# Two chunks per turn of the main loop of a retention-and-SoLU kernel, with a new order of its ends

## The chip, the core and the metric

One of the eight cores of a Trainium2 chip runs the whole kernel. A core has a matrix engine (TensorE, PE in the profile, with its weight loads as PEld), three engines for elementwise work (VectorE or DVE, ScalarE or ACT, GpSimd or POOL) and SyncE (SP), which here only issues DMAs. Each engine works through its own queue in order. Matrix products land in PSUM, which has eight banks; everything else works in SBUF. The metric is the time of one execution on the device, in microseconds (us).

## What is computed

q, k and v have 8 batches, 8 heads, 576 positions and 64 columns. Retention weights the scores of a head by a power of that head's gamma, with nothing from later positions; the result of all heads, 512 wide, goes through a SoLU layer, a layer norm and a second matrix.

```
scores = q @ k.T / sqrt(64)
gamma  = 1 - 2 ** (-5 - head)
ret    = (scores * where(i >= j, gamma ** (i - j), 0)) @ v
x      = ret, heads side by side                # 4608 x 512
h      = x @ w_in                               # 4608 x 1024
e      = exp(h - max(h));  solu = h * e / sum(e)
ln     = (solu - mean) / sqrt(var + 1e-6) * g_ln
out    = ln @ w_out                             # 4608 x 512
```

## The kernel before

The 4608 positions are cut into 36 chunks of 128. Batches go in pairs: chunks of the two batches alternate for four chunks each, and the last 64 positions of both make a ninth, joint chunk (position 4 in its batch). Along a batch a state (a 64 by 64 matrix per head) is carried from chunk to chunk, so a chunk depends on the chunk two before it.

The whole order of work is written by hand. START, LOOP and END are lists of tokens `name:chunk:engine`; `run` goes through a list and calls the function of that name, and each engine's queue gets its instructions in the order of the list. START names its chunks outright; LOOP is run once for each i from FIRST, with chunk numbers counted from i; END counts from the last chunk, 35. The letter at the end picks the engine where a step can run on several: a for ScalarE, v for VectorE, g for GpSimd.

The steps of one chunk, with their lines in the profile:

- `ld` loads q, k and v (SP, L169). `cq` and `cv` scale q and v by powers of gamma and make them half precision (L176), `ck` casts k (L160).
- `tq` transposes q and k on PE (L199), `eq` copies the result to SBUF (L160). `sc` multiplies keys and queries, head by head (L223: 64 rows of the array per product, two products side by side), `mk` puts the triangular mask on, in two instructions on DVE (L236).
- `kv` makes the chunk's product of keys and values (L247: 64 columns of the array per product), `ad` adds it to the state on DVE (L260, L262), `dk` and `d3` scale the state on POOL (L274, L286). The joint chunk has none of these.
- `av` multiplies the masked scores by v (L298: 64 columns), `fs` adds the part that comes from the state (L313: the full array); `ex` copies the sum to SBUF (L160).
- `m1` is the product with w_in (L345, eight products of 512 columns), `mx` its negative maximum (DVE, L355), `xp` the exponential (ACT, L361), `so` h times e with its sum (DVE, L370), `ce` takes the mean off (DVE, L379 and L384, in place), `sq` sums the squares (ACT, L393), `rt` makes the row factor on POOL in three small instructions (L402, L405, L406).
- `tu` transposes the result (L414), `eu` copies it to SBUF (L160), `m2` multiplies by w_out (L428), `st` scales the output (ACT, L436) and stores it (SP, L441).

`mr` is a piece of `m1` used at the start, when the rows of w_in come in one after the other; `hm` to `hw` do the last chunk in halves; `li`, `wi`, `lo`, `wo` load the weights and make them half precision; `wu` is a dummy product.

PSUM is shared out by hand too: `m1` has two slots of two banks, and all other products take one of four single banks, in the order in which the digits of BANKS name them. A product waits until the last user of its bank has been read.

Before, FIRST is 7, STEP 1 and STOP 32: a turn of the loop is one chunk's worth of every step, taken from different chunks, and there are 25 turns.

Of the kernel before, what the change touches and what calls it, by code (L numbers as in the profile page):

```python
# [10 lines left out]
FP = mybir.dt.float32  # L11
F16 = mybir.dt.float16
P = 128
H = 8
D = 64
# [1 line left out]

FIRST = 7  # L20
STEP = 1
STOP = 32
START = """
ld:1 c1:0 cq:1:g ck:1:a tq:1 ld:0 ld:2 cq:2:g eq:1:v ck:0:v ck:2:g cv:0:v cq:0:v sc:1 li:3
mk:1 tq:0 cv:1:g eq:0:v sc:0 kv:0 mk:0 kv:1 av:1 wi:3:0:a tq:2 cv:2:g kv:2 ad:1 eq:2:v
wi:3:1:g li:2 li:0 d3:1 dk:1 li:1 ad:0 fs:1 av:0 ld:4 ld:3 ex:1:a wi:0:1:v wi:2:1:v wi:2:0:v
fs:0 mr:1:3 wi:1:1:g d3:0 sc:2 ex:0:v wi:0:0:a mk:2 mr:1:0 mr:1:2 wi:1:0:a mr:1:1 mr:0:0
cq:4:g ck:4:a ad:2 mr:0:2 dk:0 mx:1 mr:0:1 ld:5 tq:4 eq:4:v mr:0:3 xp:1 d3:2 av:2 sc:4 fs:2
c2:0 wu:0:5 cv:4:g mx:0 ex:2:a cq:3:g ld:6 so:1 xp:0 ck:3:a ce:1 sq:1 lo:2 kv:4 m1:2 mk:4 so:0
dk:2 tq:3 av:4 eq:3:a cv:3:g kv:3 fs:4 ex:4:a ck:5:a cq:5:g mx:2 tu:1 cv:5:g tq:5 xp:2 ad:4  # L30
lo:1 eu:1:a sc:3 ad:3 ce:0 m1:4 mk:3 av:3 cq:6:g eq:5:a so:2 ck:6:a dk:3 d3:3 fs:3 mx:4 ex:3:a
d3:4 cv:6:g sc:5 tq:6 sq:0 d3:6 kv:5 m1:3 ce:2 lo:3 lo:0 eq:6:a tu:2 dk:4 mk:5 ad:5 sc:6 kv:6
wo:5:g av:5 xp:4 wo:4:a fs:5 mk:6 eu:2:a ld:7 so:4 ex:5:a wo:3:a wo:7:a tu:0 av:6 eu:0:v
wo:2:a wo:1:a ce:4 d3:5 wo:6:g cq:7:g rt:1 sq:4 wo:0:v rt:0 cv:7:g sq:2 fs:6 rt:4 m1:5 tu:4
mx:3 ad:6 xp:3 m2:0 eu:4:v ld:8 ld:9 ex:6:a m2:1 dk:5 mx:5 cq:8:g m2:4 ck:7:v so:3 tq:7 dk:6
ce:3 tu:3 xp:5 st:0 m1:6 kv:7 so:5 sq:3 eq:7:v ck:8:v eu:3:v sc:7 ad:7 ce:5 ld:10 st:1 mx:6
ld:11 st:4 tq:8 rt:2 ld:12 cv:8:v eq:8:a mk:7 m2:2 m2:3 ck:9:a sc:8 xp:6 rt:3 st:2 av:7 cq:9:g
mk:8 cq:10:g fs:7 st:3 ex:7:a ck:10:v cv:9:g
"""
LOOP = """  # L40
tu:-2 so:-1 tq:2 dk:0 d3:0 eq:2:a eu:-2:a ce:-1 m1:0 kv:1 ad:1 av:1 sc:2 mx:0 sq:-2 mk:2 fs:1
ex:1:a rt:-2 cq:4:g xp:0 ld:6 m2:-2 st:-2 cv:3:v ck:4:g
"""
END = """
d3:-3 dk:-3 so:-4 cv:0:g tq:-1 m1:-3 eq:-1:a d3:-2 kv:-2 av:-2 ad:-2 sq:-5 sc:-1 fs:-2 mk:-1
tq:0 ex:-2:a tu:-5 eq:0:a mx:-3 eu:-5:a m1:-2 kv:-1 ce:-4 mx:-2 xp:-3 av:-1 fs:-1 ex:-1:a
so:-3 m2:-5 sc:0 kv:0 ad:-1 ce:-3 dk:-2 xp:-2 mk:0 so:-2 rt:-5 m1:-1 av:0 dk:-1 sq:-4 mx:-1
st:-5 sq:-3 fs:0 ex:0:a tu:-3 rt:-4 tu:-4 hm:0:0 eu:-4:a ce:-2 hm:0:1 eu:-3:a xp:-1 tu:-2
rt:-3 hx:0:0 m2:-3 hx:0:1 hp:0:0 eu:-2:v m2:-4 hp:0:1 st:-3 so:-1 ce:-1 sq:-2 ho:0:1 ho:0:0
tu:-1 rt:-2 d3:-1 m2:-2 hc:0 sq:-1 eu:-1:v ht:0:1 st:-4 ht:0:0 rt:-1 hq:0:0:v m2:-1 he:0:0:v  # L50
he:0:1:a hq:0:1:a st:-2 st:-1 rt:0 h2:0:0 hw:0:0:a h2:0:1 hw:0:1:v ad:0
"""

BANKS = """
012301230130120123010230213103210231230231203012303120312013201302130210321032013201302130210321
032013201302130210321032013201230123021302132013201230123021302132013201230123021302132013203120
3123012301320132031203123012301320132013021301203123030213013
"""


# [25 lines left out]
def kernel(  # L86
# [66 lines left out]
    def bank(shape, dtype, name):  # L153
        return ps.tile(shape, dtype, tag="b" + next(banks), name=name)

    ENG = {"a": nc.scalar, "v": nc.vector, "g": nc.gpsimd}
    T = {}
# [78 lines left out]
            nc.vector.tensor_tensor(out=r, in0=s, in1=m, op=ALU.mult)  # L236
            T["ret", n].append(r)

    def kv(n):

        k16, v16 = T.pop(("k16", n)), T["v16", n]
        if chunks[n][1] == 4:
            return
        kp = bank([P, 4, D], FP, "kp")
        for hp in range(4):
            for e in range(2):
                nc.tensor.matmul(  # L247
                    out=kp[64 * e : 64 * e + 64, hp], lhsT=k16[:, 2 * hp + e],
                    rhs=v16[:, 2 * hp + e], start=True, stop=True,
                )  # L250
        T["kp", n] = kp
# [370 lines left out]
    def run(order, base):  # L622

        for token in order.split():
            name, n, *more = token.split(":")
            n = base + int(n)
            if 0 <= n < NCH:
                step[name](n, *more)

    with tc.manual_schedule():  # L630
        run(START, 0)
        for i in range(FIRST, STOP - STEP + 1, STEP):
            run(LOOP, i)
# [31 lines left out]
```

## Time and profile before

| | us |
|---|---|
| median of 3 runs | 223.36 (222.85 to 224.05) |
| the profiled execution, its own time | 223.33 |
| its span in the profile | 221.5 |
| PE busy in it | 203.6 (92%) |
| DVE busy | 196.2 (89%) |
| ACT busy | 186.6 (84%) |
| POOL busy | 163.8 (74%) |
| mean granted clock of TensorE | 0.998 |

The span runs from the first to the last instruction in the profile; the device's own time is 1.8 us more. Busy shares are sums over stages, and neighbouring instructions of one engine overlap a little at their ends, so an instruction's cost to its engine is best read from its start to the start of the next where nothing is waited for.

### The profile page before, as it was taken

To read this page: it belongs to the slowest core of one execution; us is meant where nothing else is said; L and a number is where in the kernel's file an instruction comes from. 1 tells how busy PE (TensorE), PEld (TensorE's weight loads), DVE (VectorE), ACT (ScalarE), POOL (GpSimd) and SP (SyncE) were. 2 spreads that over 40 slices of the span, in tenths; PEclk is the share of its full clock that TensorE was granted. 3 is DMA by queue.
4 is the path that set the end of the run, shared out by engine and by line. 5 is a ranking of instruction groups with operands and counts; after the bars stand their busy time and mean duration, and the time that the engine had idled before them with its cause. 6 is when DMAs were issued, how large, how long until landed. Compare 5 with 4: busy or idle time off the path is not lost.

```text
span 221.5 us, 5624 instructions
## 1 busy us (share of the span) xinstructions
PE 203.6 (92%) x2125; PEld 117.8 (53%) x2125; DVE 196.2 (89%) x343; ACT 186.6 (84%) x294; POOL 163.8 (74%) x245
## 2 busy tenths in 40 slices
PE   0269989999999999999999999999999999999992
PEld 0144455555655555555555555555555555554552
DVE  0288899999899999999999999999999999989970
ACT  2112799997899999999999999999999999998982
POOL 2077879699659988887759988887759988895050
PEclk9999999999999999999999999999999999999999
DMA  7999999889999996999897967998897945111024
GB/s 150 212 307 307 206 226 337 207 177 254 269 241 262 215 244 158 247 250 223 174 241 176 209 140 188 256 204 191 183 207 174 210 99 143 50 47 52 0 96 142
DMA packets 121084, 42.50 MB, mean 192 GB/s; under 512 B 114657, under 2 KB 115041, under 8 KB 121057
## 3 DMA queue, kind: packets, MB, share of 16 engines
q1 hardware_dynamic: 119424, 41.82, 81.5%
q10 hardware_dynamic: 1632, 0.32, 0.9%
q8 instruction: 16, 0.26, 0.6%
q14 instruction: 12, 0.09, 0.2%
HBM read 32.70 MB, written 9.44 MB: 190 GB/s over the span
## 4 chain that ended last, share of the span: by engine, by line
PE 81%; DVE 6%; SPq 6%; DMA 4%; issue 1%; ACT 0%; DVEq 0%
PE o L428 27%; PE h L345 24%; PE lp L414 7%; PE tp L199 6%; PE sc L223 5%; SPq L169 5%; PE x L313 4%; DMA kf<-in_k_dram 4%; PE x L298 4%; PE kp L247 3%; DVE ret L236 1%; DVE u L370 1%; DVE nm L355 1%; DVE u L384 1%; SPq L590 1%
## 5 line engine op out<-in xcount | busy, mean ns | idle before, releaser
L428 PE MATMUL o<-w_out,uT 128*128 128x512 f16 x280 | 65.5, 379 | 0.2
L345 PE MATMUL h<-w_in,xT 128*128 128x512 f16 x264 | 62.4, 379 | 0.2 <-DVE u L370 0.2
L236 DVE TENSOR_TENSOR ret<-sc,tris 128x512 f16<-128x512 f32 x72 | 46.1, 681 | 1.7 <-PE sc L223 1.6
L176 POOL TENSOR_TENSOR q<-qf,small 128x512 f16<-128x512 f32 x35 | 36.9, 1056 | 12.1 <-DMA qf<-in_q_dram 11.9
L361 ACT ACTIVATE e<-h,nm 128x1024 f32<-128x1024 f32 x35 | 39.1, 1117 | 4.8 <-DVE nm L355 4.6
L370 DVE SCALAR_TENSOR_TENSOR u<-h,e 128x1024 f16<-128x1024 f32 x35 | 42.4, 1211 | 0.4 <-ACT e L361 0.4
L355 DVE TENSOR_REDUCE nm<-h 128x1 f32<-128x1024 f32 x35 | 42.6, 1216 | 0.1
L428 PEld LDWEIGHTS <-uT 128*128 128x128 f16 x280 | 26.2, 98 | 26.5
L393 ACT ACTIVATE sq<-u 128x1024 f16<-128x1024 f16 x35 | 37.4, 1068 | 0.9 <-DVE u L384 0.8
L345 PEld LDWEIGHTS <-xT 128*128 128x128 f16 x264 | 24.3, 98 | 23.9 <-issue 0.2
L274 POOL TENSOR_TENSOR s<-t,small 128x512 f16<-128x512 f32 x32 | 33.7, 1054 | 2.5 <-DVE nmu L379 2.5
L160 ACT COPY qkT<-tp 128x1024 f16<-128x1024 f16 x31 | 31.4, 1012 | 3.0 <-PE tp L199 2.2
L160 ACT COPY uT<-lp 128x1024 f16<-128x1024 f16 x30 | 30.4, 1018 | 0.3 <-PE lp L414 0.3
L405 POOL TENSOR_TENSOR w<-w,ss 128x1 f32<-128x1 f32 x36 | 6.8, 190 | 29.3 <-ACT sq L393 28.4
L160 POOL CAST k<-kf 128x512 f16<-128x512 f32 x26 | 27.4, 1054 | 0.2 <-DMA kf<-in_k_dram 0.2
L436 ACT ACTIVATE o_sb<-o,rs 128x512 f32<-128x512 f32 x35 | 23.7, 680 | 0.6 <-PE o L428 0.4
L199 PE MATMUL tp<-ident,q 128*128 128x128 f16 x144 | 14.6, 226 | 8.8 <-POOL q L176 5.1
L406 POOL TENSOR_TENSOR rs<-w,mhalf 128x1 f32<-128x1 f32 x36 | 20.6, 571 | 2.8
L160 ACT CAST xT<-x 128x512 f16<-128x512 f32 x35 | 20.5, 585 | 2.5 <-PE x L313 2.3
L176 DVE TENSOR_TENSOR v<-vf,small 128x512 f16<-128x512 f32 x27 | 21.9, 812 | 0.8 <-DMA vf<-in_v_dram 0.8
L414 PEld LDWEIGHTS <-u 128*128 128x128 f16 x280 | 18.3, 98 | 6.9 <-issue 0.2
L414 PE MATMUL lp<-ident,u 128*128 128x128 f16 x280 | 21.2, 219 | 0.0
(70 smaller groups left out, 264.1 us busy)
## 6 DMA issues: line engine op xcount, KB each, us to landing
qf<-in_q_dram SPq DMA_DIRECT2D x32, 256.0 KB, 4.3
kf<-in_k_dram SPq DMA_DIRECT2D x32, 256.0 KB, 4.9
vf<-in_v_dram SPq DMA_DIRECT2D x32, 256.0 KB, 4.8
out_dram<-o_sb SPq DMA_DIRECT2D x32, 256.0 KB, 3.0
w_in<-in_moe_w_in_dram SPq DMA_DIRECT2D x4, 512.0 KB, 5.6
w_out<-in_moe_w_out_dram SPq DMA_DIRECT2D x4, 512.0 KB, 7.8
qf<-in_q_dram SPq DMA_DIRECT2D x8, 128.0 KB, 3.6
kf<-in_k_dram SPq DMA_DIRECT2D x8, 128.0 KB, 3.5
```

The source lines that it names most:

```text
L160: (engine.copy if engine is nc.scalar else engine.tensor_copy)(out=out, in_=in_)
L176: engine.tensor_tensor(out=dst, in0=T.pop((key, n)), in1=table.unsqueeze(2).to_broadcast([P, H, D]), op=ALU.mult,)
L199: nc.tensor.transpose(out=tp[:, i, hp], in_=s2[:, hp * P : (hp + 1) * P], identity=ident)
L236: nc.vector.tensor_tensor(out=r, in0=s, in1=m, op=ALU.mult)
L274: nc.gpsimd.tensor_tensor(out=s16, in0=t.unsqueeze(2).to_broadcast([P, 4, 2, D]), in1=gd.unsqueeze(3).to_broadcast([P, 4, 2, D]), op=ALU.mult,
L345: nc.tensor.matmul(out=h[:, i * 512 : (i + 1) * 512], lhsT=xT[:, d], rhs=w_in16[:, d, i * 512 : (i + 1) * 512], start=d == 0, stop=d == 3,)
L355: nc.vector.tensor_reduce(out=nm, in_=T["h", n], axis=AX.X, op=ALU.max, negate=True)
L361: nc.scalar.activation(out=e, in_=T["h", n], func=ACT.Exp, bias=T.pop(("nm", n)), accum_out=s)
L370: nc.vector.scalar_tensor_tensor(out=u, in0=T.pop(("h", n)), scalar=1.0, in1=T.pop(("e", n)), op0=ALU.mult, op1=ALU.mult, accum_out=su,)
L393: nc.scalar.activation(out=s, in_=T.pop(("v", n)), func=ACT.Square, accum_out=ss)
L414: nc.tensor.transpose(out=lp[:, c], in_=u[:, c * P : (c + 1) * P], identity=ident)
L428: nc.tensor.matmul(out=o, lhsT=uT[:, c], rhs=w_out16[:, c], start=c == 0, stop=c == NF - 1)
```

## The change

A turn of the loop takes two chunks, i + 1 and i + 2 (STEP 2, ten turns from 9 to 27). Products that use the array in the same shape stand side by side: `kv` and `av` of both chunks, then the full-array steps, then `sc` of both chunks between the two `m1`. The `kv` of the second chunk writes the second half of the bank that the first one took. The engines of some steps change: in a turn the scaling of v goes from DVE to POOL, and one of two `ex`, one of two `eq` and one of two `eu` go from ACT to DVE; one of two `ck` goes from POOL to ACT. START now covers the first nine chunks and END the last six, both in a new order (among others, a quarter of w_in is loaded ahead of the first chunk), with a new list of banks.

```diff
-FIRST = 7
-STEP = 1
-STOP = 32
+FIRST = 9
+STEP = 2
+STOP = 29
 START = """
-ld:1 c1:0 cq:1:g ck:1:a tq:1 ld:0 ld:2 cq:2:g eq:1:v ck:0:v ck:2:g cv:0:v cq:0:v sc:1 li:3
-mk:1 tq:0 cv:1:g eq:0:v sc:0 kv:0 mk:0 kv:1 av:1 wi:3:0:a tq:2 cv:2:g kv:2 ad:1 eq:2:v
-wi:3:1:g li:2 li:0 d3:1 dk:1 li:1 ad:0 fs:1 av:0 ld:4 ld:3 ex:1:a wi:0:1:v wi:2:1:v wi:2:0:v
-fs:0 mr:1:3 wi:1:1:g d3:0 sc:2 ex:0:v wi:0:0:a mk:2 mr:1:0 mr:1:2 wi:1:0:a mr:1:1 mr:0:0
-cq:4:g ck:4:a ad:2 mr:0:2 dk:0 mx:1 mr:0:1 ld:5 tq:4 eq:4:v mr:0:3 xp:1 d3:2 av:2 sc:4 fs:2
-c2:0 wu:0:5 cv:4:g mx:0 ex:2:a cq:3:g ld:6 so:1 xp:0 ck:3:a ce:1 sq:1 lo:2 kv:4 m1:2 mk:4 so:0
...
+li:2 c1:0 ld:0 cq:0:v ck:0:g tq:0 ld:1 li:1 ck:1:a cv:0:g wi:2:1:g ld:2 eq:0:a li:0 wi:2:0:v
+cq:1:v tq:1 cv:1:v sc:0 mk:0 kv:1 eq:1:v sc:1 mk:1 kv:0 av:0 wi:1:0:g wi:1:1:g cq:2:g av:1
+ad:1 cv:2:g ad:0 ck:2:a d3:0 fs:0 li:3 fs:1 dk:1 ex:1:v tq:2 mr:1:2 mr:1:1 ex:0:v eq:2:a
+wi:0:0:a sc:2 ld:4 dk:0 cq:4:g wi:3:1:a ld:3 kv:2 wi:3:0:v d3:1 wi:0:1:a mr:1:0 ck:4:a mr:0:1
+mr:1:3 cv:4:g mr:0:2 ad:2 mr:0:0 mr:0:3 mk:2 dk:2 mx:1 wu:0:3 tq:4 d3:2 av:2 fs:2 ld:5 ck:3:g
+cq:3:g mx:0 xp:1 ld:6 so:1 eq:4:a cv:3:g cq:5:g ex:2:a sc:4 ce:1 kv:4 m1:2 ck:5:g tq:3 xp:0
+mk:4 ad:4 av:4 mx:2 lo:2 fs:4 sq:1 so:0 eq:3:a sc:3 ex:4:a xp:2 lo:3 c2:0 cv:5:g kv:3 ce:0
+ad:3 d3:4 mk:3 sq:0 tq:5 m1:4 av:3 cq:6:g fs:3 tu:0 d3:3 eq:5:a ck:6:a tq:6 lo:1 ex:3:a sc:5
+so:2 rt:0 mx:4 ce:2 eq:6:a m1:3 mk:5 dk:3 sc:6 kv:5 mk:6 dk:8 eu:0:a cv:6:g tu:1 ad:5 xp:4
+wo:5:a lo:0 so:4 dk:4 wo:7:g av:5 fs:5 ex:5:a kv:6 wo:6:v wo:2:g tu:2 av:6 ad:6 eu:1:a wo:3:a
+fs:6 wo:4:a wo:0:a ex:6:a m1:5 ce:4 wo:1:v mx:3 tu:4 ld:7 eu:4:v xp:3 ld:8 ld:9 mx:5 m2:1 rt:1
...
 LOOP = """
-tu:-2 so:-1 tq:2 dk:0 d3:0 eq:2:a eu:-2:a ce:-1 m1:0 kv:1 ad:1 av:1 sc:2 mx:0 sq:-2 mk:2 fs:1
-ex:1:a rt:-2 cq:4:g xp:0 ld:6 m2:-2 st:-2 cv:3:v ck:4:g
+ld:7 kv:1 kv:2:s ad:2 ad:1 av:1 av:2 dk:1 cv:4:g fs:1 tq:3 tq:4 ex:1:v fs:2 so:0 eq:3:v eq:4:a
+ce:0 ld:8 rt:-1 m1:1 mx:1 sc:3 sc:4 ex:2:a m1:2 sq:0 mk:4 tu:0 d3:1 mx:2 xp:1 eu:0:a dk:2 so:1
+m2:-1 d3:2 ck:6:a xp:2 cv:3:g ce:1 st:-1 cq:5:g rt:0 m2:0 tu:1 st:0 mk:3 ck:5:g eu:1:v cq:6:g
+sq:1
 """
 END = """
...
+ck:-1:g tq:-3 kv:-5 ck:0:g kv:-4 av:-5 fs:-5 cq:0:g ad:-5 eq:-3:v ex:-5:a cq:-1:g tq:-2 av:-4
+sc:-3 m1:-5 eq:-2:a ad:-4 d3:-4 so:-6 mk:-3 fs:-4 cv:-2:g rt:-7 tq:-1 ex:-4:a sc:-2 mx:-5
...
+st:-5 tu:-3 eu:-4:a hm:0:0 ce:-2 mx:-1 hm:0:1 eu:-3:v hx:0:0 sq:-2 tu:-2 hx:0:1 xp:-1 eu:-2:v
+m2:-4 so:-1 ce:-1 hp:0:0 m2:-3 rt:-2 st:-4 hp:0:1 sq:-1 ho:0:0 ho:0:1 tu:-1 m2:-2 eu:-1:a hc:0
+ht:0:0 st:-3 st:-2 d3:-1 ht:0:1 hq:0:0:v he:0:0:v m2:-1 rt:-1 hq:0:1:a rt:0 he:0:1:v st:-1
+h2:0:0 h2:0:1 hw:0:0:a hw:0:1:v ad:0
 """
...
-    def kv(n):
+    def kv(n, share=""):
 
         k16, v16 = T.pop(("k16", n)), T["v16", n]
         if chunks[n][1] == 4:
             return
-        kp = bank([P, 4, D], FP, "kp")
+        if share and ("kp2", n - 1) in T:
+            kp = T.pop(("kp2", n - 1))[:, 1]
+        else:
+            T["kp2", n] = bank([P, 2, 4, D], FP, "kp")
+            kp = T["kp2", n][:, 0]
```

More of the change, by code (lines that the diff above doesn't have):

```diff
@@ L29 @@
-c2:0 wu:0:5 cv:4:g mx:0 ex:2:a cq:3:g ld:6 so:1 xp:0 ck:3:a ce:1 sq:1 lo:2 kv:4 m1:2 mk:4 so:0
[L30 to L38, printed above, removed]
+li:2 c1:0 ld:0 cq:0:v ck:0:g tq:0 ld:1 li:1 ck:1:a cv:0:g wi:2:1:g ld:2 eq:0:a li:0 wi:2:0:v
+cq:1:v tq:1 cv:1:v sc:0 mk:0 kv:1 eq:1:v sc:1 mk:1 kv:0 av:0 wi:1:0:g wi:1:1:g cq:2:g av:1
@@ new lines @@
+so:2 rt:0 mx:4 ce:2 eq:6:a m1:3 mk:5 dk:3 sc:6 kv:5 mk:6 dk:8 eu:0:a cv:6:g tu:1 ad:5 xp:4
+wo:5:a lo:0 so:4 dk:4 wo:7:g av:5 fs:5 ex:5:a kv:6 wo:6:v wo:2:g tu:2 av:6 ad:6 eu:1:a wo:3:a
+fs:6 wo:4:a wo:0:a ex:6:a m1:5 ce:4 wo:1:v mx:3 tu:4 ld:7 eu:4:v xp:3 ld:8 ld:9 mx:5 m2:1 rt:1
+cq:7:g ck:7:g sq:2 xp:5 m2:0 dk:6 st:1 ld:11 ld:10 so:3 tq:7 m1:6 eu:2:v eq:7:v cq:8:g sc:7
+sq:4 ce:3 ck:8:a m2:2 rt:2 dk:5 mk:7 d3:7 cv:7:g tq:8 d3:5 kv:7 mx:6 av:7 cv:8:g fs:7 st:0
+cq:9:g ld:13 ck:9:g rt:4 ad:7 tu:3 eq:8:v cv:9:g m2:4 so:5 st:2 ex:7:v sc:8 sq:3 tq:9 ce:5
@@ L39 @@
+mk:8 m1:7 eq:9:v ld:12 tu:5 mx:7 eu:3:a rt:3 kv:9 xp:6 m2:3 st:4 ad:9 so:6 kv:8 eu:5:a cq:10:v
+xp:7 av:8 ce:6 dk:7 ck:10:g sc:9 st:3 fs:8 m2:5 ex:8:a tu:6 tq:10 sq:5 cq:11:v cv:11:g mk:9
+m1:8 ld:15 d3:6 so:7 ad:8 ld:14 rt:5 av:9 sq:6 ce:7 d3:9 ck:11:g eq:10:a sc:10 eu:6:v m2:6
+st:5 sq:7 tu:7 ck:13:g fs:9 mx:8 ex:9:v rt:6 mk:10 xp:8 tq:11 st:6 so:8 rt:7 m1:9 eq:11:a
+sc:11 eu:7:a ce:8 mx:9 ck:12:a tu:8 m2:7 xp:9 eu:8:v st:7 cv:10:g cq:13:g dk:9 sq:8 cq:12:g
+mk:11 d3:8
 """
 LOOP = """
-tu:-2 so:-1 tq:2 dk:0 d3:0 eq:2:a eu:-2:a ce:-1 m1:0 kv:1 ad:1 av:1 sc:2 mx:0 sq:-2 mk:2 fs:1
@@ L42 @@
-ex:1:a rt:-2 cq:4:g xp:0 ld:6 m2:-2 st:-2 cv:3:v ck:4:g
+ld:7 kv:1 kv:2:s ad:2 ad:1 av:1 av:2 dk:1 cv:4:g fs:1 tq:3 tq:4 ex:1:v fs:2 so:0 eq:3:v eq:4:a
+ce:0 ld:8 rt:-1 m1:1 mx:1 sc:3 sc:4 ex:2:a m1:2 sq:0 mk:4 tu:0 d3:1 mx:2 xp:1 eu:0:a dk:2 so:1
+m2:-1 d3:2 ck:6:a xp:2 cv:3:g ce:1 st:-1 cq:5:g rt:0 m2:0 tu:1 st:0 mk:3 ck:5:g eu:1:v cq:6:g
+sq:1
 """
 END = """
-d3:-3 dk:-3 so:-4 cv:0:g tq:-1 m1:-3 eq:-1:a d3:-2 kv:-2 av:-2 ad:-2 sq:-5 sc:-1 fs:-2 mk:-1
-tq:0 ex:-2:a tu:-5 eq:0:a mx:-3 eu:-5:a m1:-2 kv:-1 ce:-4 mx:-2 xp:-3 av:-1 fs:-1 ex:-1:a
@@ L47 @@
[L47 to L51, printed above, removed]
+ck:-1:g tq:-3 kv:-5 ck:0:g kv:-4 av:-5 fs:-5 cq:0:g ad:-5 eq:-3:v ex:-5:a cq:-1:g tq:-2 av:-4
@@ new lines @@
+sc:-3 m1:-5 eq:-2:a ad:-4 d3:-4 so:-6 mk:-3 fs:-4 cv:-2:g rt:-7 tq:-1 ex:-4:a sc:-2 mx:-5
+m2:-7 ce:-6 xp:-5 eq:-1:a cv:-3:g mk:-2 tu:-6 so:-5 m1:-4 kv:-2 eu:-6:a st:-7 dk:-5 ce:-5
+ad:-2 d3:-2 cv:-1:v sq:-6 kv:-3 dk:-4 av:-3 av:-2 d3:-5 fs:-3 tq:0 ex:-3:a dk:-2 fs:-2 ad:-3
+mx:-4 sc:-1 eq:0:a m1:-3 sc:0 mk:-1 tu:-5 d3:-3 xp:-4 m2:-6 ex:-2:v so:-4 eu:-5:a rt:-6 ce:-4
+dk:-3 sq:-5 m1:-2 sq:-4 kv:-1 cv:0:g mk:0 mx:-3 kv:0 ad:-1 rt:-4 st:-6 av:-1 mx:-2 xp:-3 dk:-1
+av:0 fs:-1 so:-3 ex:-1:a xp:-2 tu:-4 rt:-5 ce:-3 sq:-3 m2:-5 fs:0 m1:-1 rt:-3 ex:0:a so:-2
@@ L52 @@
+st:-5 tu:-3 eu:-4:a hm:0:0 ce:-2 mx:-1 hm:0:1 eu:-3:v hx:0:0 sq:-2 tu:-2 hx:0:1 xp:-1 eu:-2:v
+m2:-4 so:-1 ce:-1 hp:0:0 m2:-3 rt:-2 st:-4 hp:0:1 sq:-1 ho:0:0 ho:0:1 tu:-1 m2:-2 eu:-1:a hc:0
+ht:0:0 st:-3 st:-2 d3:-1 ht:0:1 hq:0:0:v he:0:0:v m2:-1 rt:-1 hq:0:1:a rt:0 he:0:1:v st:-1
+h2:0:0 h2:0:1 hw:0:0:a hw:0:1:v ad:0
 """
 BANKS = """
-012301230130120123010230213103210231230231203012303120312013201302130210321032013201302130210321
-032013201302130210321032013201230123021302132013201230123021302132013201230123021302132013203120
@@ L57 @@
-3123012301320132031203123012301320132013021301203123030213013
+012302312301320213021302131023123012302132103103213012031203120302130210302130201313123012303121
+212031203012121230123031212102310232101010321032310101023102321010103210323101010231023210101032
+10323101010231032013012013021301302013201302121301203
 """
```

## The prediction

> **What bounds the kernel now.** I read the chain that ended last first. It lies on PE for four fifths of the span:
>
> ```profile
> PE 81%; DVE 6%; SPq 6%; DMA 4%; issue 1%; ACT 0%; DVEq 0%
> ```
>
> Then the sums by stretches: from 78 to 126.5 us, nine turns of the old loop, PE is busy 48.43 of 48.50 us, DVE 46.85, ACT 46.49, POOL 40.34. So a turn takes 48.5 / 9 = 5.39 us, two turns 10.78, and nothing but PE's own work sets it. The timeline of PE shows one turn (start, duration, engine, line):
>
> ```profile
> 101.16 1.89 PE L345 MATMUL h<-w_in,xT 128*128 128x512 f16 x8
> 102.97 0.32 PE L247 MATMUL kp<-v,k 128*64 128x64 f16 x8
> 103.12 0.39 PE L298 MATMUL x<-ret,v 128*64 128x128 f16 x8
> 103.45 0.40 PE L223 MATMUL sc<-qkT 64*128 64x128 f16 x8
> 103.78 0.40 PE L313 MATMUL x<-qkT,s 128*128 128x128 f16 x4
> 104.01 1.89 PE L428 MATMUL o<-w_out,uT 128*128 128x512 f16 x8
> 105.74 0.61 PE L414 MATMUL lp<-ident,u 128*128 128x128 f16 x8
> ...
> 106.63 1.89 PE L345 MATMUL h<-w_in,xT 128*128 128x512 f16 x8
> ```
>
> Starts count, not durations. Eight transposes take 0.45 (105.74 to 106.19), 0.056 each. The eight half-width products of L298 run two at a time, so 4 x 0.056 = 0.22 is due, but 0.33 passes until L223, and 0.33 again until L313; the four of L313 take their 0.23. L345 takes 1.81 before a 64-column group, L428 1.73 before a full one. Each change of array shape thus costs about 0.10, three times a chunk.
>
> DVE is only a little less loaded. Its timeline, same turn:
>
> ```profile
> 101.30 1.21 DVE L370 SCALAR_TENSOR_TENSOR u<-h,e 128x1024 f16<-128x1024 f32 x1
> 102.44 0.08 DVE L370 DVE_READ_ACCUMULATOR u<-h,e 128x1 f32 x1
> 102.55 0.15 DVE L379 TENSOR_SCALAR nmu<-su 128x1 f32<-128x1 f32 x1
> 102.74 0.49 DVE L384 TENSOR_SCALAR u<-u,nmu 128x1024 f16<-128x1024 f16 x1
> 103.40 0.42 DVE L262 TENSOR_TENSOR t<-kp,s 128x256 f32<-128x256 f32 x1 [0.18 <-POOL w L402]
> 103.74 1.21 DVE L355 TENSOR_REDUCE nm<-h 128x1 f32<-128x1024 f32 x1
> 104.87 1.28 DVE L236 TENSOR_TENSOR ret<-sc,tris 128x512 f16<-128x512 f32 x2
> 106.07 0.78 DVE L176 TENSOR_TENSOR v<-vf,small 128x512 f16<-128x512 f32 x1
> ```
>
> From start to start: `so` 1.25, the two halves of `ce` 0.19 and 0.41 (108.21 to 108.62 a turn on), `ad` 0.34, `mx` 1.13, `mk` 1.20, `cv` 0.70. That is 5.2 of 5.4.
>
> **The change, part by part.** *PE in the loop.* Per two chunks the shapes change four times in place of six (into `kv`/`av`, out, into `sc`, out): 0.2 less, so PE alone would need 10.78 - 0.20 = 10.58. Side by side, the second `kv` uses no bank of its own; the products are the same eight, 0.15.
>
> *DVE in the loop.* A turn keeps two each of `ad`, `so`, `ce`, `mx`, `mk` (0.67 + 2.50 + 1.20 + 2.26 + 2.40 = 9.03), loses both `cv`, and takes one `ex`, `eq` and `eu`. These DVE forms stand elsewhere in the trace: `ex` 19.48 to 20.08, `eq` 23.34 to 23.95, `eu` 0.60. Sum 9.03 + 1.81 = 10.84. This is above PE's 10.58 and no less than the old 10.78: DVE becomes the bound, and PE's 0.2 is worth nothing in the loop.
>
> *Can DVE run without gaps?* I laid out a turn by hand, with 0.20 from the end of a PE group to DVE's start (the transposes at 22.91 end at 23.14, DVE copies at 23.34) and 0.13 from DVE's end to PE's start (copy at 7.41 plus 0.61, `sc` at 8.16). With the turn's first `kv` at 0: `eu` 0.20, `ad` 0.80, `ex` 1.47, `so` 2.07, `eq` 3.32, `ce` 3.93, `mx` 4.52, `mk` 5.65, `mx` 6.85, `so` 7.98, `ce` 9.23, `mk` 9.83 to 11.03. PE: `fs` 0.90 to 1.12, `m1` 2.30 (after `ex`), `sc` 4.16 (after `eq`), `m1` 4.70, `tu` 6.43, `m2` 6.98, `m2` 8.71, `tu` 10.43 to 10.88. The first `m2` takes the bank of the second `sc` and waits 0.1 for `mk`; the next `eu` waits for the last `tu` until 11.08. So the turn is 11.08 - 0.20 = 10.88. The next `av` needs the last `mk` at 11.16 and comes at 11.24.
>
> *ACT* has 2 `xp` 2.2, 2 `sq` 2.1, `eq`, `eu` 1.8, `ex` 0.5, `ck` 0.5, 2 `st` 1.4: 8.5, off the path. The closest: `st` frees the bank of the second `av` at 11.36, 0.1 before it is due.
>
> *POOL* has, start to start, 2 `cq`, 2 `cv`, 2 `dk` at 1.0, `ck` and 2 `d3` at 0.57, 2 `rt` at 1.14: 10.0 of 10.88. It starts `dk` at 1.60, behind `ad`, ends the last `cq` near 11.8, and takes up the next `dk` at 12.48. Cover 0.65; beyond that `dk`, `fs` and `tq` come late. Its `rt` waits for `sq`, with `cv`, `cq` queued behind; `sq` is 2 us early.
>
> *Loads and stores.* Per two chunks the same six loads and two stores. SP now issues both chunks' loads together, behind a store that waits for the turn's last `st`. A chunk's q is used over 15 us later, and loads land 4.3 to 4.9 us after issue: nothing. If late, POOL's queue stops at `cq`.
>
> *The loop:* ten turns of 10.88, less 0.6 where the joint chunks have no `ad`: 108.2 against 20 x 5.39 = 107.8. **+0.4**, at best -0.3 (DVE's 10.84 with no wait, less the 0.6). Worst: as the port rival below.
>
> *What DVE's moves do to POOL.* The trace shows `ce` held up by POOL, and not always:
>
> ```profile
> 26.53 1.35 DVE L384 TENSOR_SCALAR u<-u,nmu 128x1024 f16<-128x1024 f16 x1
> ...
> 48.09 0.49 DVE L384 TENSOR_SCALAR u<-u,nmu 128x1024 f16<-128x1024 f16 x1
> ```
>
> POOL at these times:
>
> ```profile
> 25.55 1.04 POOL L176 TENSOR_TENSOR q<-qf,small 128x512 f16<-128x512 f32 x1
> 26.55 1.04 POOL L274 TENSOR_TENSOR s<-t,small 128x512 f16<-128x512 f32 x1
> ...
> 47.80 0.81 POOL L406 TENSOR_TENSOR rs<-w,mhalf 128x1 f32<-128x1 f32 x1
> ```
>
> Behind a full-size operation `ce` takes 1.35, 0.86 over its 0.49; inside the one-element L406 nothing, and L406 is stretched instead. In my turn the two `ce` (4.11, 9.42) fall into POOL's two `rt` (3.60 to 4.74, 8.87 to 10.0). I take no loss. The page "SBUF — State Buffer" of the Trainium skill, section "SBUF: two separate sides", says that whichever of the two starts first keeps the shared ports for its whole instruction. The first row agrees, the second does not; by the page both `ce` would wait for what is left of `rt`, up to 0.5 each, and the loop would lose up to 10 us.
>
> *START.* The shape changes per chunk stay outside the loop (62 in START and END; the old order had 119 in all, 60 of them in 20 loop chunks): **+0.3**. The dummy products (three for five) lie in PE's wait for `so` of chunk 1 before `m1` of chunk 2: nothing. The same 13 loads stand ahead of the last quarter of w_in as before (20 us), so the end of chunk 1's `m1` stays; only the first product comes later. From that `so` (26.3) to `m1` of chunk 5, DVE sets the pace: 13.6 us of DVE work in the new order (3 `ce`, 4 `mk`, 3 `ad`, 2 `mx`, 3 `so`), so 40.1 with the 0.2 to PE; before it was 41.21, with about 1.1 of waits behind POOL. POOL now has more to do, so most of these waits should remain: **-0.3**, between -1.1 and, if the weights ahead of chunk 0 set the pace, +1.5 (a quarter takes 1.4 to 2.5: w_in casts at 15.91, 18.46, 19.86).
>
> *END.* Before, PE waits 0.7 near 203.5 us, for masks of the last chunk. The new order has `mk` of it 2 us early by the sums (DVE 15.8 us into END, PE needs it at 17.8), and its tail from `hm` on is the old one: **-0.7**, between -1.0 and +1.0.
>
> Sum against the profiled run's own 223.33 (median 223.36): +0.4 + 0.3 - 0.3 - 0.7 = -0.3, **223.0 us**.
>
> **Rivals.** *The port between DVE and POOL (slower).* If POOL's phase slips by half a us, `ce` falls into the full-size operations around `rt`. These cover 6.1 of 10.88 us with a mean wait of 0.4: 0.2 per `ce`, 0.45 a turn, +4.5, 227.5 us. It decides from 0.15 a turn on. For it: DVE and POOL are now both near full. Against it: `dk` waits for `ad` every turn and ties POOL to DVE.
>
> *PE stays the bound (faster).* The turn would be 10.58, -2.0 for the loop, 220.6 us with the ends as above. Against it stands the DVE sum; for it, that DVE has slack in START (its tokens at the costs above: 57.1 us of DVE work, 53.5 of PE's, begun while PE still waited for data) and could go ahead; but the banks let it lead by a fraction of a us.
>
> *START stalls on its first data (slower).* +1.5 in place of -0.3, 224.8, and a little more for a DVE that enters the loop late: 225 us. For it: until 20 us the loads run without a break. Against: the bytes ahead of `m1` are the same.
>
> *The ends gain more (faster).* START's 1.1 of waits goes whole and the loop runs at 10.84: 221.8.
>
> **How the numbers follow.** About 0.5%, 1.1 us, is what a measurement can tell from no change. DVE-bound loop with small gains at the ends 0.36 (221.6 to 224.6), port 0.22, PE bound 0.12, START stall 0.15, better ends 0.15. Faster by over 0.5% (below 222.2): 0.12 + 0.15 x 0.7 + 0.36 x 0.2 = 0.30. Slower (above 224.5): 0.22 x 0.9 + 0.15 x 0.8 + 0.36 x 0.15 = 0.37. Within: 0.33. The range from 220.5 to 228 leaves out a tenth above (a port that costs more than a mean phase) and a tenth below (a loop at PE's pace with better ends too).
>
> **What would show it.** Right: PE shows gaps of about 0.3 a turn before `m2` or `m1`, DVE none; turns of 10.85 to 10.95 between first `kv`s; L384 at 0.49 through the loop; `m1` of chunk 5 near 41 us. Wrong: PE without gaps and turns of 10.6 (DVE's sum is too high), or L384 above 0.7 on average (the port), or a first `m1` after 20 us.

## The result: 1.3% slower

| | before | after |
|---|---|---|
| median, us | 223.47 (222.85 to 224.05, 6 runs) | 226.28 (225.8 to 227.22, 6 runs) |
| ratio | | 1.0131, 95% interval 1.0101 to 1.0160 |
| the profiled execution, us | 223.33 | 226.25 |
| its span | 221.5 | 224.5 |
| first product / `m1` of chunk 5 / last product | 5.12 / 41.21 / 217.3 | 6.98 / 42.09 / 220.3 |
| changes of array shape | 119 | 102 |

The predicted time was 223.0 us with a range of 220.5 to 228.0: the time lies in the range, 3.3 us above the forecast, and on the side to which I gave 0.37.

The chain that ended last shows at once what kind of loss it is. Before, PE held 81% of it, DVE 6%. After:

```profile
PE 58%; DVE 27%; SPq 4%; POOL 4%; issue 3%; DMA 2%; ACT 1%; DVEq 0%; POOLq 0%
```

The kernel now waits for other engines in places where it did not. To see where, I added up, from the start of each product to the start of the next, what a product needs (0.216 us for 512 columns, 0.056 for 128 and in proportion for 64, half where two run side by side), 0.095 for each change of shape, and called the rest idle:

| PE idle, us | before | after |
|---|---|---|
| from the first product to `m1` of chunk 5 | 14.1 | 13.4 |
| from there to 75 us | 0.5 | 1.2 |
| 75 to 185 us (the loop) | 1.6 | 4.7 |
| 185 us to the end | 1.2 | 1.3 |

Up to `m1` of chunk 5 the kernel loses 0.9 us (the first product is 1.9 later; less idle time and two dummy products fewer give half of it back). Behind it 3.9 us of idle time are new. There the shape changes fall from 90 to 71, which gives 19 x 0.095 = 1.8 us. The sum, 0.9 + 3.9 - 1.8 = 3.0, is the difference of the spans.

One plain turn on PE, from the timeline (start, duration, engine, line):

```profile
85.39 0.44 PE L262 MATMUL kp<-v,k 128*64 128x64 f16 x16
85.66 0.67 PE L313 MATMUL x<-ret,v 128*64 128x128 f16 x16
86.27 0.40 PE L328 MATMUL x<-qkT,s 128*128 128x128 f16 x4
86.50 0.39 PE L210 MATMUL tp<-ident,q 128*128 128x128 f16 x4
86.72 0.39 PE L210 MATMUL tp<-ident,k 128*128 128x128 f16 x4
87.00 0.38 PE L210 MATMUL tp<-ident,q 128*128 128x128 f16 x4
87.22 0.39 PE L210 MATMUL tp<-ident,k 128*128 128x128 f16 x4
87.44 0.39 PE L328 MATMUL x<-qkT,s 128*128 128x128 f16 x4
87.66 1.89 PE L360 MATMUL h<-w_in,xT 128*128 128x512 f16 x8
89.49 0.62 PE L234 MATMUL sc<-qkT 64*128 64x128 f16 x16
90.04 1.90 PE L360 MATMUL h<-w_in,xT 128*128 128x512 f16 x8
91.78 0.61 PE L429 MATMUL lp<-ident,u 128*128 128x128 f16 x8
92.22 3.62 PE L443 MATMUL o<-w_out,uT 128*128 128x512 f16 x16
```

The next turn starts at 96.22: 10.83 us. Two plain turns of the old loop take 10.95 between their `kv` (5.48 each, rounded). So a plain turn did become cheaper. The one gap that recurs stands ahead of the second pair of transposes: groups of four take 0.22, but 0.28 passes from 86.72 to 87.00; a turn later it is 0.11 more than the products need. DVE in the same turn:

```profile
85.50 0.69 DVE L171 COPY uT<-lp 128x1024 f16<-128x1024 f16 x1
86.11 0.75 DVE L277 TENSOR_TENSOR t<-kp,s 128x256 f32<-128x256 f32 x2
...
94.60 0.49 DVE L399 TENSOR_SCALAR u<-u,nmu 128x1024 f16<-128x1024 f16 x1
95.00 1.28 DVE L247 TENSOR_TENSOR ret<-sc,tris 128x512 f16<-128x512 f32 x2
96.33 0.69 DVE L171 COPY uT<-lp 128x1024 f16<-128x1024 f16 x1
```

It has hardly a gap either; only the last `mk` takes 1.33 until the next `eu` where two cost 1.20, 0.13 of waiting.

From one turn's first `kv` to the next, the ten turns take 10.73, 10.84, 10.84, **11.10**, **10.96**, 10.92, 10.84, 10.84, **11.62** and **11.59** us (the last holds 0.45 of END's transposes). The dear ones are the turns of 16/17 and 26/27, which hold a joint chunk, and those of 18/19 and 28/29, which hold first chunks of a batch (10/11 holds one too and is not dear). In the turn of chunks 26 (joint) and 27, on DVE, POOL and PE:

```profile
165.73 1.23 DVE L399 TENSOR_SCALAR u<-u,nmu 128x1024 f16<-128x1024 f16 x1
166.88 1.21 DVE L370 TENSOR_REDUCE nm<-h 128x1 f32<-128x1024 f32 x1
168.01 1.27 DVE L247 TENSOR_TENSOR ret<-sc,tris 128x512 f16<-128x512 f32 x2
```

```profile
165.63 1.04 POOL L187 TENSOR_TENSOR v<-vf,small 128x512 f16<-128x512 f32 x1
```

```profile
168.75 0.61 PE L429 MATMUL lp<-ident,u 128*128 128x128 f16 x8 [0.51 <-DVE ret L247]
```

The joint chunk has no `dk` and no `d3`, POOL runs ahead, its scaling of v starts 0.1 before `ce`, and `ce` takes 1.23 for 0.49. The mask behind it is late, and `tu`, which needs the bank that the mask empties, stands for 0.51 by the row, 0.67 by starts. A part of this turn's loss comes from the turn before it: chunks 24 and 25 have no `d3`, a cast on POOL starts just ahead of `ce`, `ce` takes 0.85, and the first `av` of the turn of 26/27 waits 0.33 by starts for the mask behind it:

```profile
160.03 0.61 POOL L171 CAST k<-kf 128x512 f16<-128x512 f32 x1
160.08 0.85 DVE L399 TENSOR_SCALAR u<-u,nmu 128x1024 f16<-128x1024 f16 x1
162.18 0.64 PE L313 MATMUL x<-ret,v 128*64 128x128 f16 x16 [0.15 <-DVE ret L247]
```

In the turn of chunks 16 and 17 it is the joint chunk 17 itself: its `fs` needs the state that `dk` of chunk 16 makes in the same turn.

```profile
108.97 0.19 PE L328 MATMUL x<-qkT,s 128*128 128x64 f16 x1
109.37 0.38 PE L328 MATMUL x<-qkT,s 128*128 128x64 f16 x7 [0.20 <-POOL s L289]
```

In the turn of chunks 18 and 19 there is no `fs`, so the second pair of transposes comes early, and waits half a us for the bank of `kv`, until DVE has read both halves:

```profile
119.97 0.38 PE L210 MATMUL tp<-ident,q 128*128 128x128 f16 x4 [0.35 <-DVE t L275]
```

The turn of 28/29 has no `fs` for chunk 28, and its second pair of transposes waits 0.31 by starts (174.94).

And START begins later:

```profile
6.98 0.61 PE L210 MATMUL tp<-ident,q 128*128 128x128 f16 x4 [6.98 <-DVE q L187]
```

### The profile page after: what moved, and what is told of

It reads as the page before. It is cut to its first block, busy times and chain, and to the rows that moved or that the text cites. A ratio compares the mean times of both kernels' runs of the same rounds, so it can differ in the third digit from the quotient of the medians.

```text
span 224.5 us, 5615 instructions
## 1 busy us (share of the span) xinstructions
PE 203.5 (91%) x2123; PEld 118.6 (53%) x2123; DVE 200.1 (89%) x353; ACT 165.8 (74%) x267; POOL 171.1 (76%) x262
## 4 chain that ended last, share of the span: by engine, by line
PE 58%; DVE 27%; SPq 4%; POOL 4%; issue 3%; DMA 2%; ACT 1%; DVEq 0%; POOLq 0%
PE o L443 19%; PE h L360 17%; DVE ret L247 6%; DVE u L385 5%; PE lp L429 5%; DVE nm L370 5%; PE tp L210 4%; SPq L180 3%; PE sc L234 3%; DVE u L399 3%; PE x L313 3%; DMA w_in<-in_moe_w_in_dram 2%; PE x L328 2%; DVE t L277 2%; PE kp L262 2%
## 5 line engine op out<-in xcount | busy, mean ns | idle before, releaser
L443 PE MATMUL o<-w_out,uT 128*128 128x512 f16 x280 | 64.3, 379 | 0.0
L408 ACT ACTIVATE sq<-u 128x1024 f16<-128x1024 f16 x35 | 36.9, 1054 | 9.6 <-DVE u L399 9.5
L187 POOL TENSOR_TENSOR v<-vf,small 128x512 f16<-128x512 f32 x34 | 35.8, 1052 | 3.0 <-DMA vf<-in_v_dram 3.0
L187 POOL TENSOR_TENSOR q<-qf,small 128x512 f16<-128x512 f32 x32 | 34.1, 1068 | 1.3 <-DMA qf<-in_q_dram 1.2
L171 ACT COPY qkT<-tp 128x1024 f16<-128x1024 f16 x21 | 21.2, 1009 | 10.6 <-PE tp L210 10.5
L171 ACT COPY uT<-lp 128x1024 f16<-128x1024 f16 x19 | 19.2, 1012 | 5.4 <-PE lp L429 5.2
L399 DVE TENSOR_SCALAR u<-u,nmu 128x1024 f16<-128x1024 f16 x35 | 20.0, 573 | 1.2
L420 POOL TENSOR_TENSOR w<-w,ss 128x1 f32<-128x1 f32 x36 | 9.2, 255 | 14.7 <-ACT sq L408 12.3
L171 POOL CAST k<-kf 128x512 f16<-128x512 f32 x20 | 12.5, 629 | 9.0 <-DMA kf<-in_k_dram 9.0
```

The source lines that it names most:

```text
L171: (engine.copy if engine is nc.scalar else engine.tensor_copy)(out=out, in_=in_)
L187: engine.tensor_tensor(out=dst, in0=T.pop((key, n)), in1=table.unsqueeze(2).to_broadcast([P, H, D]), op=ALU.mult,)
L399: nc.vector.tensor_scalar(out=u, in0=u, scalar1=nmu, scalar2=None, op0=ALU.add, op1=ALU.bypass)
L408: nc.scalar.activation(out=s, in_=T.pop(("v", n)), func=ACT.Square, accum_out=ss)
L443: nc.tensor.matmul(out=o, lhsT=uT[:, c], rhs=w_out16[:, c], start=c == 0, stop=c == NF - 1)
```

## The experiments

The questions were these. Does the quarter of w_in ahead of the first chunk cost the time at the start? Is the plain turn of 10.84 set by DVE's own sum, as I forecast, or by PE's work and its wait for the bank of `kv`? And are the dear turns a matter of DVE's load, or of POOL's phase beside `ce`? All ratios are to the kernel before, which ran on the same chip. They go by all executions, while the times are medians, so a ratio can differ from the quotient of the two medians by up to 0.3%.

### The weights behind the first chunks

```diff
-li:2 c1:0 ld:0 cq:0:v ck:0:g tq:0 ld:1 li:1 ck:1:a cv:0:g wi:2:1:g ld:2 eq:0:a li:0 wi:2:0:v
-cq:1:v tq:1 cv:1:v sc:0 ...
+c1:0 ld:0 cq:0:v ck:0:g tq:0 ld:1 li:2 li:1 ck:1:a cv:0:g ld:2 eq:0:a li:0
+cq:1:v tq:1 cv:1:v wi:2:1:g sc:0 ... ad:0 wi:2:0:v ...
```

> The changed kernel with one thing undone in START: the first quarter of w_in is loaded behind the first two chunks again, not ahead of them (its two casts move back accordingly). Theory A (the weights ahead of chunk 0 set START back): the first product comes at 5.1 us in place of 6.98, the product with w_in of chunk 5 near 41 us in place of 42.09, the time falls by 1.0 to 1.5 us to about 225.0. Rival (the bytes ahead of the first product with w_in are the same, so only the first transposes come earlier): no change, 226.3, chunk 5 at 42.

Measured: 225.47 us, ratio 1.0073 (1.0054 to 1.0093). The first product is 2.2 us earlier and `m1` of chunk 5 starts at 40.69 in place of 42.09:

```profile
4.81 0.61 PE L210 MATMUL tp<-ident,q 128*128 128x128 f16 x4 [4.81 <-DVE q L187]
```

The loop's turns are as without the edit (10.73, 10.84, 10.84 up to 11.63 and 11.60). So 0.6% of the 1.3% lies in the place of this one load with its two casts. The `so` of chunk 1 shows where the time goes; in the changed kernel, and with the load moved back:

```profile
26.36 1.22 DVE L385 SCALAR_TENSOR_TENSOR u<-h,e 128x1024 f16<-128x1024 f32 x1
```

```profile
25.12 1.22 DVE L385 SCALAR_TENSOR_TENSOR u<-h,e 128x1024 f16<-128x1024 f32 x1
```

It ends at 27.6 in the first and at 26.3 in the second, where the old kernel has it. Of the 1.4 us by chunk 5, 0.7 is left in the span: PE idles 0.8 more between chunk 5 and the loop.

The same load was also put first in the kernel before:

```diff
-ld:1 c1:0 cq:1:g ...
+li:2 ld:1 c1:0 cq:1:g ...
```

> The kernel before with one thing of the change: the quarter of w_in that the change loads first is loaded ahead of the first chunk here too (another quarter is the first to be used). Theory A (weights ahead of the first chunk set the start back wherever they stand): +1.0 to +1.7 us on the kernel before, 224.4 to 225.1. Rival (only the changed order of START is sensitive, since there VectorE casts weights ahead of the first masks): within 0.5 us of the kernel before.

Measured: 225.61 us, ratio 1.0090 (1.0063 to 1.0117). The first product comes at 6.83, `m1` of chunk 5 at 42.76 in place of 41.21, and the old loop's turns don't change. The loss is the load's own, not the new order's around it. At 2.0 us by the ratio it is a little above the expected 1.0 to 1.7: to the 1.5 us by chunk 5 come 0.6 of idle time between there and 75 us.

### One eviction back to ACT

```diff
-... tq:3 tq:4 ex:1:v fs:2 ...
+... tq:3 tq:4 ex:1:a fs:2 ...
```

> The changed kernel with one step of the loop turned back: the copy of the attention result of the first chunk of a turn goes to ScalarE, not VectorE (0.60 us of VectorE a turn). Theory A (VectorE's own 10.84 us set the turn): turns of 10.6 us where they were 10.84, the loop 2.0 to 2.6 us shorter, about 224.0 us. Rival (POOL, or its hold on the port, sets the turns): turns stay at 10.8, 226.3 us, and the means of L399 rise.

Measured: 224.96 us, ratio 1.0053 (1.0033 to 1.0072). DVE is relieved of 0.60 a turn and now stands idle in a plain turn, waiting for `m1`:

```profile
89.96 1.23 DVE L370 TENSOR_REDUCE nm<-h 128x1 f32<-128x1024 f32 x1 [0.33 <-PE h L360]
```

Yet plain turns still take 10.84. So DVE's load is not what holds them there. The rival's two signs both come, turns that stay and a higher mean of `ce` (563 ns over the loop in place of 543; in most turns one of the two takes 0.57 to 0.64, beside the end of a scaling on POOL), though the time falls. Whether POOL sets the plain turn is decided further down, where the same `ce` go with turns of 10.74. The gain comes from the dear turns: 18/19 falls from 10.96 to 10.62, 26/27 from 11.62 to 10.66, the last from 11.59 to 11.29; the first rises from 10.73 to 11.00.

### The two `sc` apart again

```diff
-... mx:1 sc:3 sc:4 ex:2:a m1:2 ...
+... mx:1 sc:4 ex:2:a m1:2 sc:3 ...
```

(with the banks of the two exchanged.)

> The changed kernel with the grouping of scores undone in the loop: the scores of one chunk before the second product with w_in, those of the other behind it, banks swapped to suit. Two shape changes more per turn, so 0.2 us more of PE. Theory A (VectorE sets the turn): within 0.5 us of 226.3, as the added PE time lies in PE's gaps. Rival (PE still sets it): +2.0 us, 228.3.

Measured: 226.66 us, ratio 1.0133 (1.0112 to 1.0154). Two changes of shape more per turn make a plain turn 11.05, 0.21 dearer: PE's work counts in full, which it would not if DVE's sum were the bound by any margin. The total alone would have spoken for theory A, for it lies within 0.5 us of 226.3; the turns decide. The total moves less than the nine or ten turns would have it (10 x 0.21 = 2.1 us, 0.9%), for the turn of 26/27 is 10.81 here, without its long wait, and the last one stays at 11.59.

### More work for POOL

Where a chunk skips `dk` (a joint chunk) or `d3` (a joint chunk and the two before it), POOL does the same step on constants whose result nobody reads, so that its queue is as long in every turn. The diff shows the step in place of `dk`; that of `d3` is like it.

```diff
+            if 10 <= n < 30:
+                p16 = stp.tile([P, 4, 2, D], F16, tag="p16", name="p16")
+                nc.gpsimd.tensor_tensor(
+                    out=p16, in0=padt.unsqueeze(2).to_broadcast([P, 4, 2, D]),
+                    in1=gd.unsqueeze(3).to_broadcast([P, 4, 2, D]), op=ALU.mult,
+                )
...
```

> The changed kernel with dummy work on POOL: in the loop's turns where a chunk has no state to scale, POOL does the same two operations on constants into tiles that nobody reads, so that POOL's phase is the same in all turns. Theory B (in the turns of chunks 24 to 27 POOL runs ahead, the centring on VectorE falls into a full-size POOL operation and waits 0.36 and 0.75 us): L399 at 0.49 in the whole loop, turn of chunks 26 and 27 at 10.9 in place of 11.6, 0.7 to 1.2 us off, 225.3 us, although POOL does more. Rival (POOL's load itself is what makes these turns long): +0.5 to +1.5 us.

Measured: 225.24 us, ratio 1.0072 (1.0050 to 1.0093). Work that nobody needs makes the kernel 0.6% faster. In the turn of 26/27, on DVE and POOL:

```profile
165.39 0.49 DVE L411 TENSOR_SCALAR u<-u,nmu 128x1024 f16<-128x1024 f16 x1
```

```profile
163.82 1.04 POOL L188 TENSOR_TENSOR v<-vf,small 128x512 f16<-128x512 f32 x1
164.84 0.27 POOL L429 TENSOR_SCALAR w<-s 128x1 f32<-128x1 f32 x1
165.19 0.19 POOL L432 TENSOR_TENSOR w<-w,ss 128x1 f32<-128x1 f32 x1
```

`ce` again falls beside the one-element instructions, the turn takes 10.75 in place of 11.62, and the mean of `ce` over the loop is 487 ns in place of 543. The other turns stay as they were, up to 0.13. So the loss in this turn is POOL's phase, as in the port rival, but in one turn of ten.

### The state products between the transposes

If the wait for the bank of `kv` sets the plain turn, then the second `fs`, put ahead of the second pair of transposes, covers it.

```diff
-... fs:1 tq:3 tq:4 ex:1:v fs:2 so:0 ...
+... fs:1 tq:3 fs:2 tq:4 ex:1:v so:0 ...
```

> The changed kernel with only the state product of the second chunk moved between the two transpose groups. Theory A (in the changed kernel VectorE's own work of 10.84 sets the plain turns, and PE's gap ahead of the second transposes is only where the lag shows): plain turns stay at 10.84, the gap moves elsewhere, 226.3 us within 0.5. Rival (the wait for the shared bank sets them): plain turns of 10.73 to 10.76, 225.4 us.

Measured: 225.35 us, ratio 1.0078 (1.0059 to 1.0097). Three of the four plain turns take 10.75 to 10.79, that of 24/25 takes 10.93, with DVE's work unchanged. Most of what the total gains comes from the turn of 26/27, which takes 10.62 here in place of 11.62. In a plain turn DVE's last `mk` goes straight into the next `eu`:

```profile
105.66 1.27 DVE L247 TENSOR_TENSOR ret<-sc,tris 128x512 f16<-128x512 f32 x2
106.89 0.69 DVE L171 COPY uT<-lp 128x1024 f16<-128x1024 f16 x1
```

So DVE's own sum is 10.72 at most, and the rest of the 10.84 was the bank. In the turn of 16/17 the edit does harm, for there `fs` of the joint chunk waits all the longer (0.83 between these two starts, where it needs 0.03); the turn takes 11.54:

```profile
108.26 0.19 PE L328 MATMUL x<-qkT,s 128*128 128x64 f16 x1
109.09 0.38 PE L328 MATMUL x<-qkT,s 128*128 128x64 f16 x7 [0.64 <-POOL s L289]
```

Together with the eviction on ACT:

> Two edits of the loop: the copy of the first chunk's attention result on ScalarE, as in the run before, and the state product of the second chunk moved between the two transpose groups, so that the second group of transposes, which takes the bank that both key-value products share, starts 0.22 us later. In the run with the copy alone VectorE stood idle and the plain turns still took 10.84, with a gap of 0.10 on PE ahead of that group. Theory C (with VectorE relieved, PE's own 10.73 and the wait for the shared bank, which the two additions on VectorE must have read, make the 10.84): plain turns of 10.73 to 10.76, 0.6 to 1.0 us less than the copy alone, about 224.0 us. Rival (something else paces at 10.84, such as POOL): plain turns stay at 10.84.

Measured: 224.82 us, ratio 1.0048 (1.0029 to 1.0068). Three of the four plain turns take 10.74 and that of 24/25 takes 10.84, with DVE relieved: no lower than with DVE full. What is left is PE's own work, 10.73. The mean of `ce` is 563 ns as with the eviction alone, so POOL's hold on it is not what made the 10.84. The total falls by only 0.1 against the eviction alone, where 0.6 to 1.0 was expected, for the turn of 16/17 takes 11.55.

### All four together, and the turn of chunk 17 spared

The load, the eviction, the place of `fs` and the added work of POOL:

> All four edits together: w_in's first quarter behind the first two chunks, the copy of the first chunk on ScalarE, the state product between the transposes, dummy work that keeps POOL's phase. If the four losses are separate, they add up: 1.3 (loads) + 1.8 (copy) + 0.8 (shared bank) + 0.3 (phase, of which the copy has taken most) = 4.2 us, 222.1 us, which would be just under the kernel before (223.4). If they hide one another, 223 to 224.5 us.

Measured: 224.41 us, ratio 1.0046 (1.0020 to 1.0072), far from the sum of the four gains (0.6 + 0.8 + 0.5 + 0.6 = 2.5%). The turn of 16/17 has grown to 12.03, with a gap of 0.81 within its `fs` and another of 0.39 behind a `ce` of 0.85. So the next versions leave `fs` behind the transposes in that turn alone:

```diff
-            run(LOOP, i)
+            late = LOOP.replace("fs:2 tq:4 ex:1:a so:0", "tq:4 ex:1:a fs:2 so:0")
+            run(late if i == 15 else LOOP, i)
```

Without the added work of POOL, and with it:

> The changed kernel with four edits: the second quarter of w_in is loaded and cast behind the first two chunks, the loop's eviction of the first chunk's x goes to ACT, the second chunk's state products stand between the two pairs of transposes in every turn but the one whose second chunk is the joint chunk 17 (there they stay behind both pairs), no added GpSimd work. Theory 'each dear place has its own price': from 1.0131, 0.6% goes with the load, 0.8% with the eviction, 0.1 us in each of seven plain turns (0.3%) with the products' place: ratio 0.996 to 0.999, turn of chunks 16 and 17 at 11.1 us, turn of 26 and 27 near 10.6. Theory 'a stall that goes is replaced by the next one': the ratio stays where the sum of the edits stood with the bad turn of chunk 17 (1.0046) less that turn's 0.9 us at most, 1.0005 to 1.004, with a new wait in some other turn.

> The same four edits, and the added decays on constants in GpSimd for joint and last chunks, so that its queue is as long in every turn. If the long rescale behind full-size GpSimd work in the turn of chunks 26 and 27 is what the added work cured, and the eviction's move cured it already, this is equal to the kernel without the added work within 0.3%: 0.996 to 1.003. If the added work takes GpSimd's slack where the rescale now waits, it is slower by 0.3 us or more, seen as rescales above 800 ns in the loop.

Measured: 223.38 us, ratio 1.0019 (0.9992 to 1.0046), and 223.52 us, ratio 0.9999 (0.9983 to 1.0016). The turn of 16/17 is 11.10 and 11.20, that of 26/27 10.65 and 10.52. The added work now makes no difference: with the eviction moved, the `ce` of 1.23 is gone without it (the longest `ce` of the loop is 0.79, with the added work 0.66). Neither is faster than the kernel before.

Only the load and the eviction:

> The changed kernel with two edits only: the second quarter of w_in behind the first two chunks, and the loop's eviction of the first chunk's x on ACT. If the two prices add: 1.0131 less 0.0058 less 0.0078, ratio 0.9995. If one replaces the other: 1.004 to 1.005. Plain turns 10.84 us, the turns of chunks 18/19 and 26/27 near 10.65.

Measured: 223.90 us, ratio 1.0011 (0.9992 to 1.0030). One load with its two casts, and one eviction, account for the whole loss within what can be measured, and these two prices do add: 1.0131 - 0.0058 - 0.0078 = 0.9995 was due. The prices of the eviction, of the added work and of the place of `fs` don't add, for each of them cures the turn of 26/27.

Why the best version only breaks even shows in its sums: it keeps the 102 changes of shape (17 fewer than before, 1.6 us), and has 3.2 us of idle time in the loop where the old one has 1.6, and 1.2 against 0.5 between chunk 5 and the loop, 2.3 more together. The largest places in its loop are 0.37 before `m1` at 75.6 us, 0.37 in the `fs` of chunk 17, 0.31 before the transposes in the turn of 18/19, 0.25 before `av` in that of 26/27, and 0.34 before transposes in the last turn. No run here takes these away.

## Why the prediction failed, step by step

I forecast 0.3 us less and the kernel takes 2.8 more by the medians, 3.0 by the spans. The step that failed most is START's term: I let the end of chunk 1's `m1`, and with it the `so` at 26.3, stay where it was, and the load ahead of chunk 0 moved it by 1.3. Behind it come END, and the loop's turns with other work than the plain one.

- **Plain turns: the time right, the reason half wrong.** I forecast 10.88 and said 10.85 to 10.95; they take 10.84. But I said that DVE's sum of 10.84 sets it. That sum is 10.72 at most: `so` has 1.25 in my terms, and 0.11 of it is the wait for its own sum, which goes where another instruction stands between `so` and `ce`, as one `eq` does here (the old kernel has it too: from 29.00 to 30.14). PE's own work is 10.73, not 10.58, for I took the saved 0.20 off a mean of 10.78 that holds joint chunks, which have no `kv` and `ad`, where a plain pair took 10.95. So the two engines are level, and what makes 10.84 of 10.73 is the wait for the bank that both `kv` share. The turn that I laid out by hand does not have this wait, and the sign that I named, gaps of 0.3 before `m2` or `m1`, is not there: the gap is 0.1, before the second transposes. The rival "PE stays the bound" had the right engine with the wrong size.
- **Turns with joint or first chunks: the failed term of the loop.** I took 0.6 off for the missing `ad`. None of it came; the turns 11.10, 11.62 and the last (11.14 without END's transposes) are 0.2 to 0.7 above my 10.88 instead. Chunk 10 to chunk 30 takes 110.3 us from `kv` to `kv`, 109.8 without END's transposes, where I had 108.2. The old loop takes 108.6 over the same chunks, also more than my 107.8. I checked the plain turn by hand, and not the turns where the list does different work.
- **The port between DVE and POOL: rare.** 18 of the loop's 20 `ce` take 0.49, as forecast; two take 0.85 and 1.23. The rival's 4.5 us did not come. What I held against it, that `dk` ties POOL to DVE in every turn, holds only where there is a `dk` and a `d3`: without them POOL ran ahead. The rule of the Trainium skill's page "SBUF — State Buffer", section "SBUF: two separate sides" (whoever starts first keeps the shared ports for the whole instruction), fits the two dear cases, but for 0.2: `ce` goes on 0.2 before the recorded end of POOL's instruction. It fits the turn shown too, where `ce` at 94.60 starts first and keeps its 0.49, and POOL's one-element instruction behind it is stretched from 0.19 to 0.47:

```profile
94.32 0.26 POOL L417 TENSOR_SCALAR w<-s 128x1 f32<-128x1 f32 x1
94.66 0.47 POOL L420 TENSOR_TENSOR w<-w,ss 128x1 f32<-128x1 f32 x1
```

It does not fit where a one-element instruction starts first. In START one has run for 0.30 when `ce` starts, and it is the one-element instruction that is stretched, from 0.55 to 0.83; in four turns of the loop one has run for 0.02, with the same outcome:

```profile
42.56 0.83 POOL L421 TENSOR_TENSOR rs<-w,mhalf 128x1 f32<-128x1 f32 x1
42.87 0.49 DVE L399 TENSOR_SCALAR u<-u,nmu 128x1024 f16<-128x1024 f16 x1
```

- **START: the sign wrong, the largest miss.** Forecast -0.3, measured +0.9 by `m1` of chunk 5 and 0.7 of idle time more until the loop. I reasoned that the bytes ahead of that `m1` are the same, so only the first product would come later. But the `so` of chunk 1 ended at 27.6, not 26.3. With the load behind the first two chunks it ends at 26.3, and `m1` of chunk 5 stands at 40.69, 0.5 before the old kernel's: the rest of the term was about right, and this load undid it. The two runs on that load show that the start of chunk 5's `m1` follows the first product: 2.2 us earlier became 1.4 there, 1.7 later became 1.5 in the old kernel. The rival "START stalls on its first data" is what happened; I gave it 0.15. By the run without the load, its price is 1.4 at chunk 5 and 0.7 of the span, or 1.3 by the ratio. That START's +1.6 by these sums is near the rival's +1.5 is luck in part, for the 0.7 further on is not the load's: without the load PE idles still more there. Why the casts of the last quarter come 0.85 us later with the same bytes ahead of them (20.71 against 19.86; twelve loads in both lists, where I wrote 13) stays open.
- **END: no gain.** The wait of 0.7 near 203.5 us is gone, as forecast, but four others of 0.31, 0.23, 0.15 and 0.15 stand in its place: idle time 1.3 against 1.2, so +0.15 for -0.7. Taking away the longest wait of a stretch says nothing of the next one; that part was argued from sums of work on DVE alone. No run isolates END.
- **Shape changes.** Right: 0.095 to 0.10 each, seen again where two more a turn cost 0.21. And +0.3 outside the stretch from 75 to 185 us, behind chunk 5 (three changes), is what the sum gives.

Terms together: -0.3 - 0.7 + 0.4 + 0.3 became +1.6 + 0.15 + 1.0 + 0.3, which is 3.0 of span. (The loop's 1.0 is 3.1 of new idle time less 22 changes of shape between 75 and 185 us.)

## What to carry to other kernels

When a loop is unrolled over two items, price the irregular turns first: they come with fewer steps, which lets engines run out of the phase that made the regular turn work, so "less work" there cost up to 0.8 us a turn. When two engines are level within 1%, look at the bank or buffer between them: here it set the pace, and moving one instruction off either engine was tried more cheaply than argued. And at the start, bytes moved ahead of the first product were paid for in both kernels here, though the same bytes were due before the first large product.

## What the runs showed of the chip that I had not expected

- GpSimd's one-element instructions don't hold up a full-size rescale on VectorE, even where they start first: the 18 cheap rescales of the loop, 16 of them beside such instructions, took 0.486 to 0.491 us, and most of the one-element instructions were stretched (0.19 to 0.47, 0.26 to 0.56, 0.55 to 0.79). Full-size GpSimd work that starts first does: 0.85 beside a cast that had started 0.04 us earlier, 1.23 beside a scaling that had started 0.09 us earlier, 0.57 to 0.64 where a scaling was near its end (the kernel with the eviction on ACT). So an engine's useless work can pay, when it shifts its small instructions beside the other's large ones (0.6% here).
- The sum that `so` makes costs 0.11 us of VectorE's time only if the instruction that reads it comes next: 1.25 from start to start then, 1.14 with another instruction between (the `so` at 87.36 in the trace, whose follower, an `eq`, starts at 88.50).
- Time won or lost ahead of the first large product does not reach the end unchanged: 1.4 us won by chunk 5 became 0.7 of span, or 1.3 by the ratio; in the old kernel 1.5 lost there became 2.4 of span, or 2.0 by the ratio.
